# A linear-attention and two-MLP kernel: ScalarE's opening in another order, a 128x3 square on another engine, and the second batch's decays loaded at another point

## The chip, the cores and the metric

The kernel runs on one core of a Trainium2 chip. The metric is the device time of one execution in microseconds (us), the median over several runs. PE is TensorE, DVE is VectorE, ACT is ScalarE, POOL is GpSimd, and SP is the engine whose queue issues most of the DMAs. Each engine works through its own list of instructions in order; between engines, semaphores hold an instruction until its inputs are there.

## The reference, cut to what matters

```python
mag = sqrt(a_re**2 + a_im**2); scale = minimum(mag, 0.999) / (mag + 1e-6)
a = (a_re * scale, a_im * scale)               # complex decay, per (b, h, t, d)
for t in range(768):                           # B=4, H=8, D=48
    S = a[t] * S + k[t] v[t]^T                 # complex state, 48x48 per head
    y[t] = q[t] . Re(S)
x = y, heads side by side                      # (4, 768, 384)
u = x + token-MLP(x);  x1 = u + relu(u @ w_ch1) @ w_ch2
xn = layernorm(x1) * g_ln
out = x1 + relu(xn @ w2_ch1) @ w2_ch2
```

## The kernel before

A batch is worked in two stages. The first one (`gen_E` with `gen_A`, `gen_L2`, `gen_C`, then `gen_P`) turns the recurrence into matrix products; the second (`gen_M`) is the token MLP and the two channel MLPs.

In the first stage the 384 channels of a batch lie in three tiles of 128 partitions (i = 0, 1, 2), each in two halves of 384 time steps. Six *pieces* (tile, half) make a batch. `gen_A` first brings each decay to the right length. This is the piece's *first correction*: ACT squares the piece (L228), DVE adds the two squares, ACT takes Ln, Exp and a Square with a sum beside it (L232 to L234), and DVE finishes with three products and one 128x768 product into the decay tile `aj`. DVE then multiplies the decays together along 16 steps (`cmul`, a pair of products into `p`, then a pair of sums back into `aj`; below this is a *scan step*), and `gen_L2` joins the chunks. `gen_C` divides k by the running product and multiplies q by it, and its last two products write the four strips that SP sends, one DMA per head and strip, into the per-head tiles `stk` (L355, L356). `gen_P` then runs each head on PE: transposes of k (L425), scores (L438), state sums (L465), a scan on DVE (L466), and the outputs (L485, L497). Batch 0 goes in two parts, tiles 0 and 1 first and tile 2 behind (`PARTS`); heads 0 and 1 need only tile 0, heads 2 to 4 end in tile 1, heads 5 to 7 need tile 2.

Tile `aj` is shared by all batches. As soon as `gen_C` is through with tile i, `load_a(b + 1, i)` fetches the next batch's decays into its place (L63, 768 KB). The next batch's pieces then go through `gen_A` between the work of this batch. The scratch of the first two of them is called `t_1473` and `t_1559` in the lists below, the last tile of batch 0 works in `u`, `w_106` and `qk`.

The second stage reads weights that are split into two f16 parts on the way: POOL (and SP for the first few) loads `raw`, DVE and ACT split it (L530 to L534), 28 tiles in all. `tok1_half` is run twice: half 0 needs heads 0 to 3, half 1 heads 4 to 7. Its products go to the tile `y` (18 matmuls for j = 0, 18 for j = 1).

The program is written as generators that a driver interleaves, but the order on each engine is set by a scheduler at compile time, which estimates when each instruction can start. `tc.issue_after(x)` puts what stands under it behind instruction x on that engine. Where a queue's order in the lists below differs from the order of the code, the scheduler chose so.

Beside the result the kernel sums checks; `gstat` is the square of the layer-norm gain `gl`, three columns, compared at the very end (L1056). `gl` arrives by the 14th DMA of the SP queue.

Of the kernel before, what the change touches and what calls it, by code (L numbers as in the profile page):

```python
# [13 lines left out]
AF = mybir.ActivationFunctionType  # L14
ALU = mybir.AluOpType
PSUM = bass.MemoryType.PSUM

B, H, S, D = 4, 8, 768, 48
# [5 lines left out]
HB = S // 2  # L24
# [12 lines left out]
def tile_kernel(ctx: ExitStack, tc: tile.TileContext, a_in, qk_in, v_in, aq2_in, v2_in, wt_in, wm1_in, wm2_in, w64_in, g_in, c_in, out):  # L37
    nc = tc.nc
    V, A, T, G = nc.vector, nc.scalar, nc.tensor, nc.gpsimd
# [14 lines left out]
    def steps(x, i, half):  # L54

        if half is None:
            return x[:, :, i * S:(i + 1) * S]
        return x.rearrange("p x (i h s) -> p x i h s", i=3, h=2)[:, :, i, :, half * (HB // 2):(half + 1) * (HB // 2)]

    def load_a(b, i, half=None):  # L60
        o, s = steps(aj, i, half), steps(a_in[b], i, half)
        for x in range(2) if half is not None else (slice(0, 2),):
            nc.sync.dma_start(out=o[:, x], in_=s[:, x])  # L63
# [13 lines left out]
    gl = cp.tile([P, 3], F32, name="gl")  # L77
    nc.sync.dma_start(out=cst, in_=c_in)
    wstat = cp.tile([P, 28], F32, name="wstat")
    rstat = cp.tile([P, 6 * B], F32, name="rstat")  # L80
# [7 lines left out]
    gstat = cp.tile([P, 3], F32, name="gstat")  # L88
# [7 lines left out]
    V.memset(bias[:, 5:6], TINY)  # L96
    b_ln, b_one, b_eps, b_zero, b_eps_s, b_tiny = (bias[:, i:i + 1] for i in range(6))
    A.activation(out=eye_h, in_=eye, func=AF.Copy, scale=WS * WS)
    V.tensor_tensor(out=gstat, in0=gl, in1=gl, op=ALU.mult)

    w1 = ap.tile([P, FT, 4 * DM], F16, name="w1")
    w1_f = w1.rearrange("p k s -> p (k s)").bitcast(F32)
# [20 lines left out]
    def pair(x, n=2):  # L123
        return x.unsqueeze(1).to_broadcast([P, n] + list(x.shape[1:]))
# [29 lines left out]
    def big():  # L154
        return ap.tile([P, 6 * HB + 6], F32, tag="u", name="u", bufs=1)
# [4 lines left out]
    fin = {}  # L160
# [31 lines left out]
    def gen_E():  # L192
        V = Rec()
        nxt_q = [load_qk(0, j // 2, j % 2) for j in range(6)]
        load_w(1)
        for b in range(B):
            rec[0] = b == 0
            Ct = ap.tile([P, 3, 6 * 24], F32, tag="I", name="I")
            W = ap.tile([P, 2, 3, NCH], F32, tag="W", name="W")
            sq = ap.tile([P, 2, 3 * NCH], F32, tag="sq", name="sq")  # L200
            st = ap.tile([P, 2, 3 * NCH], F32, tag="st", name="st")
            V.memset(W[:, 0, :, 0:1], 1.0)
            V.memset(W[:, 1, :, 0:1], 0.0)
            for part in PARTS if b == 0 else ((0, 1, 2),):
                for x in gen_A(b, part):
                    yield x
                for x in gen_L2(b, part, Ct, W, sq, st):
                    yield x
                yield "C"
                for i in part:  # L210
                    for x in gen_C(b, i, Ct, st, nxt_q):
                        yield x
                    if b + 1 < B:
                        load_a(b + 1, i)
                    yield ("done", b, i)

    av = aj.rearrange("p x (j k r) -> p x j k r", j=6, k=KB)

    def gen_A(b, part):
        V = Rec()  # L220
        js = slice(2 * part[0], 2 * part[-1] + 2)
        n = 2 * len(part)
        for hf in range(2):
            for i in part:
                ah = steps(aj, i, hf)
                t = scratch(b, 2 * i + hf)
                s4, s5, s6, s7 = (t[:, j * HB:(j + 1) * HB] for j in range(4))
                A.activation(out=t[:, 0:2 * HB].rearrange("p (x h s) -> p x h s", x=2, h=2), in_=ah, func=AF.Square)  # L228
                yield "wait"
                V.scalar_tensor_tensor(out=s4, in0=s4, scalar=TINY, in1=s5, op0=ALU.add, op1=ALU.add)  # L230
                nn = s4
                A.activation(out=s5, in_=nn, func=AF.Ln)  # L232
                A.activation(out=s5, in_=s5, func=AF.Exp, scale=-0.5, bias=b_ln)
                A.activation(out=s6, in_=s5, func=AF.Square, scale=1.0 / 0.4995,  # L234
                             accum_out=rstat[:, 6 * b + 2 * i + hf:6 * b + 2 * i + hf + 1])
                if b == 0:
                    V.tensor_scalar(out=s7, in0=s5, scalar1=-EPS / 0.4995, scalar2=1.0, op0=ALU.mult, op1=ALU.add)
                else:
                    A.activation(out=s7, in_=s5, func=AF.Identity, scale=-EPS / 0.4995, bias=b_one)
                yield 470  # L240
                yield "wait"
                V.scalar_tensor_tensor(out=s4, in0=nn, scalar=-1.0, in1=s6, op0=ALU.mult, op1=ALU.mult)
                yield 470
                V.scalar_tensor_tensor(out=s5, in0=s4, scalar=3.0, in1=s5, op0=ALU.add, op1=ALU.mult)
                yield 470
                V.scalar_tensor_tensor(out=s4, in0=s5, scalar=1.0, in1=s7, op0=ALU.min, op1=ALU.mult)
                yield 470
                V.tensor_tensor(out=ah, in0=ah, in1=pair(s4.rearrange("p (h s) -> p h s", h=2)), op=ALU.mult)
                yield 870
            for j in range(max(1, hf * KB // 2), (hf + 1) * KB // 2):  # L250
                cmul(av[:, 0, js, j], av[:, 1, js, j], av[:, :, js, j], av[:, :, js, j - 1], [n, 24])
                yield 1200
        fin["scan"] = e0[-1]
        yield "L2"
# [261 lines left out]
    def load_w(n):  # L516
        while len(raws) <= n:
            m = len(raws)
            raws[m] = load_raw(m, "w2" if m in (2, 3) or 8 <= m < 16 else "tw")
# [194 lines left out]
    rs = {}  # L714

    def gen_M():
        r1 = [ap.tile([P, 2, DM], F16, tag="hid", name="hid", bufs=NHID) for _ in range(2)]
        tok1_half(0, r1)
        u = big()[:, 0:6 * HB].bitcast(F16).rearrange("p (x c s) -> p x c s", x=2, c=3)
        u_hl["uh"], u_hl["ul"] = u[:, 0], u[:, 1]  # L720
        yield "head"
        for _ in tok2(0, r1, (0,)):
            yield "tok"
        tok1_half(1, r1)
        yield "tok"
        for b in range(B):
            for _ in tok2(b, r1, (0, 1, 2) if b else (1, 2)):
                yield "tok"
            ln = iter(())
            if b == 0 and IL < FT:  # L730
                g = [mlp(wm1, 0, 0 < LNPE), mlp(wm1, 1, 1 < LNPE, ("sc", "tr", "y"))]
                for s in range(FT + 1 + IL):
                    for half in range(2):
                        if not 0 <= s - half * IL <= FT:
                            continue
                        k, acc = next(g[half])
                        if half:
                            next(ln, None)
                        if k < FT:
                            yield "step"  # L740
                        else:
                            for _ in ln:
                                pass
                            ln = gen_LN(half, acc)
                            next(ln)
            for half in range(0 if b or IL >= FT else 2, 2):
                for k, acc in mlp(wm1, half, 2 * b + half < LNPE):
                    next(ln, None)
                    if k < FT:
                        yield "step"  # L750
                for _ in ln:
                    pass
                ln = gen_LN(2 * b + half, acc)
                next(ln)
            for half in range(2):
                n = 2 * b + half
                for k, acc in mlp(wm2, half):
                    next(ln, None)
                    if half and b + 1 < B:
                        if k == 2:  # L760
                            tokw(b + 1, 0)
                        if k == K_TOK:
                            yield "x"
                            r1 = tok1(b + 1)
                    if k == FT - 3:
                        o = ap.tile([P, 3, HB], F32, tag="xc", name="o", bufs=1)
                        nc.sync.dma_start(out=o, in_=x2_d[n].rearrange("c p s -> p c s"))
                    if k < FT:
                        yield "step"
                for c in range(3):  # L770
                    t = tmp()
                    V.scalar_tensor_tensor(out=t, in0=acc[c][:, 0:HB], scalar=1 / (WS * WS), in1=rs[n], op0=ALU.mult, op1=ALU.mult)
                    V.scalar_tensor_tensor(out=o[:, c], in0=o[:, c], scalar=1 / US, in1=t, op0=ALU.mult, op1=ALU.add)
                    nc.sync.dma_start(out=out[c, :, n * HB:(n + 1) * HB], in_=o[:, c])
            yield ("done", b)
# [243 lines left out]
    for b in range(B):  # L1019
        k = 0  # L1020
        while True:
# [5 lines left out]
            x = nxt(M, "M")  # L1027
# [140 lines left out]
```

## Time and profile before

| | us |
|---|---|
| median of 3 runs | 973.39 (971.98 to 974.5) |
| the profiled execution | 972.28 |
| its span in the trace | 970.6 |
| PE busy | 834.6 |
| DVE busy | 744.1 |
| ACT busy | 496.8 |

The span is what the trace covers, from the first instruction to the last; 1.7 us of the profiled execution lie around it. Busy time alone doesn't bound the kernel: in the first 130 us PE has little to do and DVE works almost without a gap, while between 700 and 800 us PE is never idle and DVE works half of the time. So the table by stretches is the one to read, together with what each engine waited for.

### The profile page before, as it was taken

How to read it: one execution, taken by the hardware profiler on the slowest of the kernel's cores; microseconds unless marked ns; L12 is line 12 of the kernel's file. 1: busy time of each engine (PE TensorE's matmuls, PEld its weight loads, DVE VectorE, ACT ScalarE, POOL GpSimd, SP SyncE). 2: the span in 40 equal slices, each digit the busy share in tenths (PEclk: the TensorE clock that was granted, in tenths of full speed). 3: DMA queues.
4: the chain of work that ended last, by engine and by line, in shares of the span. 5: the costliest groups of instructions: out<-in, count | busy, mean ns of one | idle time of the engine just before them, and what ended most of it. 6: DMA issues, size and time to landing. Idle time of an engine off the chain costs nothing.

```text
span 970.6 us, 15833 instructions
## 1 busy us (share of the span) xinstructions
PE 834.6 (86%) x5738; PEld 570.6 (59%) x5738; DVE 744.1 (77%) x1597; ACT 496.8 (51%) x1364; POOL 59.6 (6%) x113
## 2 busy tenths in 40 slices
PE   0018989699988899999889999799999999999996
PEld 0018979356556687655556666466666666656563
DVE  6999957999997788997979999988675523264543
ACT  6014434533543459434868972574676533354532
POOL 0000101000102100001010000011000000011110
PEclk9999975799999789999899999999999999999998
DMA  8024475421447533114245120343120102255572
GB/s 283 0 57 128 160 208 164 167 79 66 153 133 225 159 107 107 64 34 130 57 118 168 32 62 1 115 127 80 55 56 25 50 1 90 86 194 195 190 239 94
DMA packets 45287, 108.28 MB, mean 112 GB/s; under 512 B 5904, under 2 KB 28560, under 8 KB 45200
## 3 DMA queue, kind: packets, MB, share of 16 engines
q1 hardware_dynamic: 36816, 61.57, 21.5%
q0 software_dynamic: 8384, 45.62, 14.2%
q8 instruction: 47, 0.77, 0.3%
q14 instruction: 40, 0.33, 0.1%
HBM read 77.20 MB, written 11.01 MB: 91 GB/s over the span
## 4 chain that ended last, share of the span: by engine, by line
PE 40%; DVE 28%; DMA 11%; issue 10%; ACT 6%; SPq 4%; POOL 0%; DVEq 0%; POOLq 0%; ACTq 0%
PE m L566 11%; PE m L567 11%; PE m L568 11%; DVE t L179 6%; DVE aj L179 4%; DVE p L179 4%; DMA stk<-t 3%; DMA stk<-qk 2%; DMA raw<-in_wm 2%; DMA aj<-in_a 2%; DVE hid L576 2%; PE sc L438 2%; SPq L355 2%; SPq L356 1%; DVE qk L179 1%
## 5 line engine op out<-in xcount | busy, mean ns | idle before, releaser
L576 DVE SCALAR_TENSOR_TENSOR hid<-m,hid 128x384 f16<-128x384 f32 x198 | 109.4, 553 | 113.4 <-ACT hid L574 112.8
L566 PE MATMUL m<-u,w 128*128 128x384 f16 x576 | 189.6, 330 | 1.5 <-DVE u L626 1.3
L567 PE MATMUL m<-u,w 128*128 128x384 f16 x576 | 189.8, 330 | 0.0
L568 PE MATMUL m<-u,w 128*128 128x384 f16 x576 | 189.7, 329 | 0.0
L574 ACT ACTIVATE hid<-m 128x384 f16<-128x384 f32 x198 | 96.0, 485 | 180.8 <-PE m L568 179.7
L567 PE MATMUL m<-hid,w 128*128 128x384 f16 x540 | 177.3, 329 | 12.3 <-DVE hid L576 12.0
L568 PE MATMUL m<-hid,w 128*128 128x384 f16 x540 | 177.0, 328 | 0.0
L568 PEld LDWEIGHTS <-w 128*128 128x128 f16 x1176 | 116.5, 99 | 89.7 <-issue 20.8
L567 PEld LDWEIGHTS <-w 128*128 128x128 f16 x1176 | 116.9, 99 | 75.1 <-issue 6.5
L566 PEld LDWEIGHTS <-w 128*128 128x128 f16 x1176 | 116.7, 100 | 75.2 <-issue 7.6
L566 PE MATMUL m<-hid,w 128*128 128x384 f16 x540 | 129.6, 328 | 2.4 <-ACT hid L574 2.1
L425 PE MATMUL tr<-cst,stk 96*128 96x96 f32 x125 | 17.1, 260 | 77.8 <-DMA stk<-qk 75.0
L179 DVE SCALAR_TENSOR_TENSOR t<-t 128x384 f32<-128x384 f32 x120 | 64.8, 549 | 8.5 <-ACT t L228 5.7
L425 PEld LDWEIGHTS tr<-cst,stk 96*128 96x128 f32 x125 | 13.9, 151 | 81.4 <-issue 71.3
L179 DVE TENSOR_TENSOR p<-aj 128x288 f32<-128x288 f32 (+2 forms) x150 | 52.7, 392 | 0.8
L179 DVE TENSOR_TENSOR t<-aj,I 128x768 f32<-128x768 f32 x40 | 36.4, 953 | 16.5 <-DMA stk<-t 11.8
L438 PE MATMUL sc<-stk 96*128 96x128 f32 x300 | 46.2, 289 | 2.7 <-DVE xc L682 1.4
L438 PEld LDWEIGHTS sc<-stk 96*128 96x128 f32 x300 | 42.3, 202 | 5.8 <-DVE r L443 1.7
L533 ACT ACTIVATE w<-raw 128x768 f16<-128x768 f32 x28 | 25.4, 906 | 30.0 <-DVE raw L531 29.8
L513 POOL DMA_DIRECT2D raw<-in_wm x48 | 25.9, 540 | 238.3 <-DVE w L534 109.0
L574 ACT ACTIVATION_READ_ACCUMULATOR hid<-m 128x1 f32 x198 | 38.5, 194 | 0.0
L546 ACT ACTIVATE sq<-sq 128x768 f16<-128x768 uint8 x28 | 23.6, 843 | 27.8 <-DVE sq L545 27.8
(268 smaller groups left out, 1670.7 us busy)
## 6 DMA issues: line engine op xcount, KB each, us to landing
raw<-in_wm POOLq DMA_DIRECT2D x48, 768.0 KB, 4.6
qk<-in_qk SPq DMA_DIRECT2D x23, 384.0 KB, 4.7
aj<-in_a SPq DMA_DIRECT2D x9, 768.0 KB, 5.0
stk<-t SPq DMA_DIRECT2D x40, 144.6 KB, 3.3
stk<-qk SPq DMA_DIRECT2D x40, 144.6 KB, 3.1
raw<-in_wt SPq DMA_DIRECT2D x6, 768.0 KB, 5.4
v<-in_v SPq DMA_DIRECT2D x32, 144.0 KB, 2.2
x_d<-xc SPq DMA_DIRECT2D x24, 192.0 KB, 2.5
```

Of the source, the lines that this page charges most:

```text
L179: r = getattr(nc.vector, n)(*a, **k)
L355: nc.sync.dma_start(out=stk[b, h][d0:d0 + m, hf], in_=R[r:r + m])
L425: T.transpose(tr[:, c * 96:(c + 1) * 96], qc(c, 1), eye[0:96, 0:96])
L438: last = T.matmul(sc[:, (c % 3) * P:(c % 3 + 1) * P], qc(c, 1), qc(c, 0), start=True, stop=True)
L513: (nc.sync if n < NSY else nc.gpsimd).dma_start(out=raw.bitcast(U8), in_=w_src[n].bitcast(U8)[:, 3:3 + 8 * S])
L533: wact[n] = A.activation(out=dst[:, :, 0], in_=w, func=AF.Copy, scale=WS).ins
L546: A.activation(out=t[:, HB:2 * HB].bitcast(F16), in_=bad_, func=AF.Copy, accum_out=wstat[:, n:n + 1])
L566: T.matmul(out_, wh, xh_, start=first, stop=False)
L567: T.matmul(out_, wh, xl_, start=False, stop=False)
L568: T.matmul(out_, wl, xh_, start=False, stop=last)
L574: A.activation(out=hl[:, 0], in_=p, func=AF.Relu, accum_out=hstat[:, n_h[0]:n_h[0] + 1])
L576: last[:] = [V.scalar_tensor_tensor(out=hl[:, 1], in0=p, scalar=0.0, in1=hl[:, 0], op0=ALU.max, op1=ALU.subtract).ins]
```

## The change

Three edits, and what the scheduler makes of them:

1. Under `tc.issue_after(fin["ln"])` the first Square of each piece of batch 0 stands behind the last Square of the piece before it. ACT takes the pieces one by one.
2. The check's square of `gl` is an ACT `Square` at the start of `gen_M` in place of a DVE product at L99.
3. For batch 0, `load_a(1, i)` is called for all three tiles when `gen_C` of tile 2 has been issued, not after each tile.

```diff
-    V.tensor_tensor(out=gstat, in0=gl, in1=gl, op=ALU.mult)
...
-                    if b + 1 < B:
+                    if b and b + 1 < B:
                         load_a(b + 1, i)
                     yield ("done", b, i)
+                if b == 0 and part[-1] == 2:
+                    for i in range(3):
+                        load_a(1, i)
...
-                A.activation(out=t[:, 0:2 * HB].rearrange("p (x h s) -> p x h s", x=2, h=2), in_=ah, func=AF.Square)
+                with (tc.issue_after(fin["ln"]) if b == 0 and "ln" in fin else ExitStack()):
+                    A.activation(out=t[:, 0:2 * HB].rearrange("p (x h s) -> p x h s", x=2, h=2), in_=ah, func=AF.Square)
...
-                A.activation(out=s6, in_=s5, func=AF.Square, scale=1.0 / 0.4995,
-                             accum_out=rstat[:, 6 * b + 2 * i + hf:6 * b + 2 * i + hf + 1])
+                fin["ln"] = A.activation(out=s6, in_=s5, func=AF.Square, scale=1.0 / 0.4995,
+                                         accum_out=rstat[:, 6 * b + 2 * i + hf:6 * b + 2 * i + hf + 1]).ins
...
     def gen_M():
+        A.activation(out=gstat, in_=gl, func=AF.Square)
```

In the lists of the changed kernel the line numbers are 1 lower from L100 on and 2 to 4 higher further down (L228 is L231, L234 is L237, L355 is L358, L376 is L379).

ACT at the program's start, before: squares of the first pieces (`t`, `u`, `t`, `w_106`) stand between the Ln, Exp and Square of the others.

```order
L228 ACTIVATE t<-aj 128x768
L228 ACTIVATE u<-aj 128x768
L232 ACTIVATE t<-t 128x384
L228 ACTIVATE t<-aj 128x768
L233 ACTIVATE t<-t,bias 128x384
L232 ACTIVATE u<-u 128x384
L228 ACTIVATE w_106<-aj 128x768
L234 ACTIVATE t,rstat<-t 128x384
L232 ACTIVATE t<-t 128x384
L233 ACTIVATE u<-u,bias 128x384
```

ACT at the same place, changed:

```order
L231 ACTIVATE t<-aj 128x768
L235 ACTIVATE t<-t 128x384
L236 ACTIVATE t<-t,bias 128x384
L237 ACTIVATE t,rstat<-t 128x384
L231 ACTIVATE u<-aj 128x768
L235 ACTIVATE u<-u 128x384
L236 ACTIVATE u<-u,bias 128x384
L98 ACTIVATE eye_h<-cst 128x128
L720 ACTIVATE gstat<-gl 128x3
L237 ACTIVATE u,rstat<-u 128x384
```

Each piece now runs to its end before the next begins, and the square of `gl` stands inside the second piece, ahead of its last Square. DVE's list follows: of the 15 scan steps of tiles 0 and 1, two stood with other work between their products and their sums before, and eight do now; the number of instructions up to the end of these steps is the same but for the square of `gl`. Before that square DVE had six instructions to do, five of 384 columns into `t`, `u` or `w` with two inputs and one with one; in the changed list eight stand ahead of the first that needs the second piece's last Square, the 768-column product of the first piece among them.

DVE where tile 1 of batch 0 is finished, before: `u` and `qk` are its first half, `w1_106` its second, `p` and `aj_69<-p` the scan of tile 2, and `t_1473` the first piece of batch 1.

```order
L179 SCALAR_TENSOR_TENSOR t_1473<-t_1473 128x384
L179 TENSOR_TENSOR aj_69<-p_974 128x2x24 x2
L179 SCALAR_TENSOR_TENSOR qk_117<-u_110 128x384
L179 SCALAR_TENSOR_TENSOR t_1473<-t_1473 128x384
L179 SCALAR_TENSOR_TENSOR w1_106<-w1_106 128x384
L179 TENSOR_TENSOR p_995<-aj_69 128x96 x2
L179 TENSOR_TENSOR u_110<-qk_117,aj_69 128x768
L179 SCALAR_TENSOR_TENSOR t_1473<-t_1473 128x384
```

DVE at the same place, changed:

```order
L178 TENSOR_TENSOR u_109<-qk_116,aj_69 128x768
L178 TENSOR_TENSOR p_950<-aj_69 128x96 x2
L178 TENSOR_TENSOR w1_105<-qk2_110,w1_105 128x384
L469 SCALAR_TENSOR_TENSOR U_504<-tr_507,dr_505 96x288
L178 TENSOR_TENSOR qk_116<-qk_116,aj_69 128x768
L178 TENSOR_TENSOR aj_69<-p_950 128x2x24 x2
L178 SCALAR_TENSOR_TENSOR qk2_110<-w1_105 128x384
L469 SCALAR_TENSOR_TENSOR U_553<-m1_556,dr_554 96x288
```

No piece of batch 1 is left there. The five products of `t_1473` and those of `t_1559` now stand among the last corrections of tile 2, three of them ahead of the very last of these.

SP where the strips of tile 1 have been sent and those of tile 2 follow, before: `v` are the loads of the heads' values, and each waits until the head three before it is through on PE.

```order
L356 DMA w_648<-qk_111 16x771
L63 DMA aj<-in_a 128x2x768
L376 DMA v<-in_v 128x288 x4
L355 DMA w_648<-w_106 32x771
L355 DMA w_1115<-w_106 48x771
L355 DMA w_1118<-w_106 48x771
```

SP at the same place, changed:

```order
L359 DMA w_646<-qk_110 16x771
L379 DMA v<-in_v 128x288 x2
L63 DMA aj<-in_a 128x2x768 x2
L379 DMA v<-in_v 128x288
L358 DMA w_646<-w_105 32x771
L358 DMA w_1112<-w_105 48x771
L358 DMA w_1115<-w_105 48x771
```

The load of tile 0, which stood some twenty DMAs earlier, and that of tile 1 now follow each other behind the values of heads 4 and 5; tile 2's load follows the strips of tile 2 in both.

On PE two things differ in this stretch: the 18 matmuls of `y` for j = 1 stood in one row with those for j = 0, ahead of the transposes of head 5, and now stand behind the first eight transposes and six score products of heads 5 and 6. The rest of the second stage has the same order up to small swaps.

## Rows read from the trace of the kernel before

**Rows 1.** Table by stretches (span; PE, PEld, DVE, ACT, POOL busy; PEclk; DMA share; GB/s).
```profile
80.00:120.00 40.00, 34.40 (x172) 33.76 (x172) 38.52 (x110) 17.18 (x38) 2.92 (x8) 1.00 0.43 131
120.00:160.00 40.00, 35.65 (x195) 33.93 (x195) 22.51 (x39) 15.86 (x38) 3.24 (x6) 0.69 0.59 179
...
700.00:800.00 100.00, 100.00 (x810) 67.23 (x809) 55.19 (x102) 59.75 (x185) 0.00 (x0) 1.00 0.12 34
```

**Rows 2.** Instructions in order of time, opening (start, us, what, idle before and its releaser).
```profile
4.14 0.84 ACT L228 ACTIVATE t<-aj 128x768 f32<-128x768 f32 x1 [1.98 <-DMA aj<-in_a]
5.02 0.56 DVE L179 SCALAR_TENSOR_TENSOR t<-t 128x384 f32<-128x384 f32 x1 [3.77 <-ACT t L228]
...
12.99 0.16 DVE L99 TENSOR_TENSOR gstat<-gl 128x3 f32<-128x3 f32 x1 [0.74 <-DMA gl<-in_g]
13.07 0.55 DVE L179 SCALAR_TENSOR_TENSOR t<-t 128x384 f32<-128x384 f32 x1
...
44.85 0.26 DVE L179 COPY I<-aj 128x192 f32<-128x192 f32 x1
```

**Rows 3.** The same view, scan steps of tiles 0 and 1.
```profile
22.24 0.61 DVE L179 TENSOR_TENSOR p<-aj 128x192 f32<-128x192 f32 x2
22.78 0.55 DVE L179 SCALAR_TENSOR_TENSOR w<-w 128x384 f32<-128x384 f32 x1
...
25.05 0.41 DVE L179 TENSOR_TENSOR aj<-p 128x96 f32<-128x96 f32 x2
25.39 0.55 DVE L179 SCALAR_TENSOR_TENSOR w<-w 128x384 f32<-128x384 f32 x1
...
30.28 0.61 DVE L179 TENSOR_TENSOR p<-aj 128x192 f32<-128x192 f32 x2
...
31.39 0.63 DVE L179 TENSOR_TENSOR p<-aj 128x192 f32<-128x192 f32 x2
```

**Rows 4.** The chain that ended last, in order of time (start, us, what).
```profile
88.49 0.47 DVE t L179
...
90.89 0.87 DVE aj L179
...
98.75 5.52 DMA aj<-in_a
```

**Rows 5.** Instructions in order of time around the heads of batch 0.
```profile
73.70 0.56 DVE L443 TENSOR_TENSOR sT<-m,cst 128x384 f32<-128x384 f32 x1 [1.11 <-PE m L438]
...
104.36 0.84 ACT L228 ACTIVATE t<-aj 128x768 f32<-128x768 f32 x1 [2.50 <-DMA aj<-in_a]
...
112.22 0.33 SPq L376 DMA_DIRECT2D v<-in_v  x1
...
127.45 0.96 DVE L179 TENSOR_TENSOR u<-u,aj 128x768 f32<-128x768 f32 x1
...
128.74 0.24 PE L566 MATMUL y<-xh,w 128*128 128x192 f16 x1 [0.90 <-DVE hid L610]
...
130.14 0.25 PE L568 MATMUL y<-xh,w 128*128 128x192 f16 x1
...
133.46 0.44 PE L425 MATMUL m<-cst,w 96*128 96x96 f32 x3 [3.07 <-DMA w<-w]
```

**Rows 6.** Table by stretches of 5 us (columns as in Rows 1).
```profile
70.00:75.00 5.00, 5.00 (x26) 5.00 (x26) 3.82 (x12) 1.34 (x3) 0.00 (x0) 1.00 0.69 183
100.00:105.00 5.00, 5.00 (x28) 5.00 (x28) 4.12 (x12) 1.74 (x3) 1.74 (x3) 1.00 0.89 293
105.00:110.00 5.00, 5.00 (x27) 5.00 (x27) 4.53 (x23) 2.92 (x7) 1.18 (x6) 1.00 0.88 344
140.00:145.00 5.00, 5.00 (x28) 5.00 (x28) 2.92 (x6) 3.26 (x7) 0.00 (x0) 0.50 0.10 38
210.00:215.00 5.00, 5.00 (x33) 3.03 (x31) 5.00 (x11) 1.99 (x5) 0.00 (x0) 1.00 0.00 0
```

**Rows 7.** The chain of waits, PE at half clock.
```profile
158.31 0.32 PE m L566
```

## The prediction

> **What bounds the kernel now.** I read the table by stretches first. From 700 to 800 us PE works all the time, so nothing done early can help or hurt there except by starting it sooner or later [rows 1]. From 80 to 120 us DVE works 38.5 of 40 us and PE waits for strips that DVE makes; from 120 to 160 DVE works 22.5 of 40 [rows 1]. So the front is DVE's, up to its last product for tile 2 of batch 0, which starts at 127.45 and ends near 128.3 [rows 5]. Then come SP's transfers, and PE starts head 5 at 133.46 after waiting 3.07 us for a strip [rows 5]. Everything behind is released by data, nothing by the clock on the wall: if head 5 starts earlier, the rest moves, unless a later wait doesn't.
>
> The second view was the instructions in order of time. In the opening the reader should look at DVE's start at 5.02 and at 13.07, from where it hardly stops until the copy at 44.85 that closes the scan [rows 2]. The third was the chain of waits: at 90.89 it goes through a 768-column product that finishes a piece of batch 1, and at 98.75 through the 5.52 us load of batch 1's next tile [rows 4]. Work of the second batch stands on the first batch's path.
>
> **The change, part by part.** All sums are made against the profiled execution, 972.28 us with a span of 970.6. That is 1.1 below the median of 973.39; I carry the differences over to the median.
>
> *Opening.* Between 5.02 and 13.07 DVE had six instructions, five of 0.47 (the 384-column step of [rows 4]) and one shorter, 2.6 us in all, so 5.4 us idle [rows 2]. In the new order ACT reaches the square of `gl` near 10.3 us: Square at 4.14, 0.84 long [rows 2], and then Ln, Exp and Square with DVE's sum between, some 3 us for each piece by the same durations. But DVE's old square started at 12.99 after waiting 0.74 for that transfer [rows 2], and SP's list is the same up to there. So ACT stands until about 13.0, and behind it in its queue the second piece's last Square and all further pieces. DVE goes on at about 13.7. It has then done eight instructions, 3.8 us, and idled 4.9. Saved: 0.5, the small square included. If `gl` cost nothing there, up to 5.4 could go; if its wait runs longer than on DVE, nothing.
>
> *Scan steps.* A step with other work between its products and its sums takes 0.54 + 0.34 = 0.88 of DVE (22.24 to 22.78, 25.05 to 25.39); alone it takes 1.11 (30.28 to 31.39) [rows 3]. Six more steps are of the first kind: 6 x 0.23 = 1.4 saved. The Trainium skill (VectorE: DVE Perf Modes, The DRAIN you can't avoid) says that a Vector instruction can't start until the pipe has emptied behind the one before, and that leaving out the wait between them saves nothing. By it both kinds of step would cost the same, and the opening would bring 0.5 and not 1.9. The two kinds of step in this trace differ by 0.23, so I keep 1.4. Opening and steps: -1.9, ends -6.8 and 0.
>
> *Batch 1's pieces leave the front.* Two pieces were finished by DVE before 128.3. Each is four steps of 0.47 and one of 0.87 [rows 4], 2.75, together 5.5. In the new list three of the 0.47 steps still stand ahead of the last product of tile 2, 1.4. So -4.1. The rest falls behind that product, in the stretch in which DVE has 17.5 of 40 us free [rows 1]; that is the cover, and without it the 4.1 comes back. Ends -5.5 and 0.
>
> *Waits that go.* DVE idled 1.18 from 70 to 75, 1.11 of it for a score product, and 0.88 and 0.47 from 100 to 110 [rows 5, 6]. The first lies where the new list puts the last sums of tile 1 ahead of the scores. The others lie where ACT stood 2.50 us for batch 1's load before its Square at 104.36 [rows 5], with a head's copy of k behind it in the queue, and PE's state sums and DVE's scan behind that. Both go: -2.5. What is late next is `t_1473`. It now stands ahead of the last products of tile 2, needs its load, and that stands behind the values of head 5, which wait until head 2 is through. In the old trace head 2 is through at 112.22, when the values of head 5 go out [rows 5]; with the gains so far (1.9 + 4.1 + 2.5) that is 103.7. The load then lands some 6 us later (5.52 at 98.75 [rows 4], and the issues ahead of it), near 110. DVE gets to `t_1473` some 6.2 us ahead of its last product (counted under B), near 113.6, so the load is there; but ACT has two Ln and two Exp of tile 2 to do ahead of its Square. I allow 0.7 for that, less than one Square. Together -1.8, ends -2.5 and +3.0 (5.5 of wait, as in B, against the 2.5).
>
> *y for j = 1.* 18 matmuls, 128.74 to 130.14 at 0.08 each [rows 5], ran while PE waited for strips and cost nothing. Now they stand among the transposes and scores of head 5, which PE works without a gap (140 to 145: 5.00 of 5) [rows 6]. 18 x 0.08 = 1.5. At half clock, 0.50 in that row, a step of 384 columns takes 0.32 [rows 7] against 5.00/33 = 0.15 at 210 us [rows 6], so it could be 2.9. It stands near the start, so I take the row at full clock: +1.5, ends 0 and 2.9.
>
> *The square of `gl` itself* is 0.16 on DVE [rows 2] and about that on ACT; beside the wait it is nothing. Three loads move as to time, none is added.
>
> Sum: -1.9 - 4.1 - 1.8 + 1.5 = -6.3. In the profiled execution's terms 966.0, at the median **967.1**.
>
> **The rivals.**
>
> *A. As summed.* About 967. Itself it goes down to 960.0, with `gl` free (-4.9) and neither the 0.7 nor the 1.5, and up to 970.4, with the scan steps' 1.4 and the opening's 0.5 lost and y at 2.9. For it: DVE leaves no slack before 128.3, and nothing behind is released by a clock. Against it: later rows are reordered by a few places as well, which can be worth a microsecond or two either way.
>
> *B. The load becomes the wait.* `t_1473` holds DVE's last products of tile 2. If heads 0 to 2 don't come earlier, the values of head 5 go out at 112.22 as before [rows 5], two loads follow, and the first lands near 118.2. ACT's 0.84 makes it 119.1, 5.5 after DVE wants it. DVE then has 6.2 us to the end of tile 2 (five of 0.47, four of 0.87, one of 0.36), 125.3 and not 128.3: -3.0, with y -1.5, **971.9**. For it: SP's order puts the loads behind values that wait for heads. Against: heads 0 to 2 depend on the same DVE list that gets 5 us shorter.
>
> *C. Hidden anyway.* From about 165 us on, splitting the weights and the second batch's scans fill DVE. If the weights' transfers set the pace there and not DVE, head 5's earlier start is lost: **973.4**. For it: weight tiles wait for buffers that heads free. Against: those heads come earlier too.
>
> *D. Slower: PE's clock.* The granted clock is 1.00 from 105 to 110 us and 0.50 from 140 to 145, PE being full in both [rows 6]; 120 to 160 has 0.69 [rows 1]. Between them lie PE's waits of 0.90 and 3.07 us [rows 5]. In that stretch the work is mostly f32, and little is lost. If the new order of waits makes the half clock last as long over f16 work, each 10 us of it do 5 us of work (0.32 against 0.15 a step). From 13 us of it on the gain is gone; 30 us of it, about what the stretch lasts now, cost 15: 967.1 + 15 = **982**. For it: a gap of PE stays ahead of head 5. Against: it stays at the same place in the order, so the slow stretch should fall on the same work. The Trainium skill (TensorE: Matmul & The Clock Gate, What's actually happening) says that activity releases the throttle; by that a PE as full as this would soon be back at full clock and D would cost a few microseconds at most. The trace has PE 5.00 of 5 busy at 0.50, which the rule doesn't explain, so I leave D its chance.
>
> **How the numbers follow.** Chances: A 0.62, B 0.13, C 0.12, D 0.13. A difference under 0.3%, 2.9 us, can't be told from none in this kernel. A lies below 970.5 whole; of B I count 0.03 as faster, 0.08 as same and 0.02 as slower, of C 0.02, 0.08 and 0.02, of D 0.03, 0.03 and 0.07. That is faster 0.70, same 0.19, slower 0.11. The range reaches from just inside A's lower end to just past C: 960.5 to 974.0. Below it I leave 0.08, above it D's tail, 0.10.
>
> **What the profile after would show.** Opening: ACT idle until about 13 ahead of the square of `gl`, DVE's closing copy near 43 in place of 44.85. If that copy comes at 40 or earlier, `gl` landed sooner than I think; at 45, the steps gained nothing. Front: no piece of batch 1 on DVE before about 112, and the last product of tile 2 ended near 121; an idle of several us ahead of `t_1473` with a load as releaser means B. PE: head 5 near 125 to 127 in place of 133.46, and the clock at 1.00 from 200 to 240. If head 5 comes that early and the end doesn't, it is C or D, and the granted clock tells which. I am wrong in kind if the time is above 973.4 with head 5 early, or if head 5 is not early at all.

## The result and the profile after

The changed kernel takes 958.37 us (median of 4 runs, 957.82 to 964.99) against 973.94 for the kernel before (4 runs, 971.98 to 975.13), a ratio of 0.9858 with a 95% interval of 0.9811 to 0.9904. The profiled executions stand at 957.82 and 972.28, spans 956.1 and 970.6: -14.5. Forecast were -6.3 and a range that ended at 960.5, so the direction was right and the forecast size less than half of the real one. Ratios here leave out runs more than 1.5% above the fastest of their kernel, which are two of frozen_y_first's six, its profiled one among them; medians count every run.

The table by stretches of the kernel after, columns as in [rows 1] (the x behind a busy time counts the records, one for each instruction that the trace holds):

```profile
80.00:120.00 40.00, 39.66 (x201) 39.60 (x202) 37.60 (x110) 15.45 (x36) 3.98 (x10) 1.00 0.58 176
120.00:160.00 40.00, 30.83 (x252) 27.36 (x251) 33.35 (x59) 22.80 (x59) 4.84 (x9) 0.87 0.84 269
```

From 80 to 120 us PE is busy 39.7 us in place of 34.4, DVE 37.6 in place of 38.5 [rows 1]; so PE had little to do only in the first 70 us, and not, as is said ahead of the prediction, in the first 130. From 120 to 160 PE does 252 records in 30.8 us where it did 195 in 35.7, and DVE works 33.4 us and not 22.5: there lies the larger part of the change.

The opening and the front of the kernel after, instructions in order of time (start, us, what, idle before and its releaser):

```profile
11.58 0.31 ACT L98 ACTIVATE eye_h<-cst 128x128 f16<-128x128 f32 x1 [1.31 <-DMA cst<-in_c]
11.79 0.19 ACT L720 ACTIVATE gstat<-gl 128x3 f32<-128x3 f32 x1
...
42.07 0.26 DVE L178 COPY I<-aj 128x192 f32<-128x192 f32 x1
...
114.72 0.84 ACT L231 ACTIVATE t<-aj 128x768 f32<-128x768 f32 x1 [1.73 <-DMA aj<-in_a]
...
115.60 0.56 DVE L178 SCALAR_TENSOR_TENSOR t<-t 128x384 f32<-128x384 f32 x1 [1.03 <-ACT t L231]
...
120.92 0.94 DVE L178 TENSOR_TENSOR u<-u,aj 128x768 f32<-128x768 f32 x1
```

The copy that closes the scan starts at 42.07 in place of 44.85 [rows 2], the last product of tile 2 at 120.92 in place of 127.45 [rows 5]. The square of `gl` waits for nothing. The new wait at `t_1473` is there, 1.03 us on DVE.

PE around the heads of batch 0, the kernel after (same columns):

```profile
121.48 0.37 PE L571 MATMUL y<-xh,w 128*128 128x192 f16 x1
127.28 0.74 PE L428 MATMUL m<-cst,w 96*128 96x96 f32 x3 [5.42 <-DMA w<-qk]
...
131.28 0.37 PE L569 MATMUL y<-xh,w 128*128 128x192 f16 x1
...
136.36 0.37 PE L500 MATMUL m<-U,w 96*128 96x48 f32 x2
136.55 0.38 PE L488 MATMUL m<-v,sT 128*128 128x48 f32 x2
...
147.84 0.41 PE L500 MATMUL m<-U,w 96*128 96x48 f32 x2
```

The same kind of products in the kernel before:

```profile
143.35 0.62 PE L485 MATMUL m<-v,sT 128*128 128x48 f32 x2
143.77 0.63 PE L497 MATMUL m<-U,w 96*128 96x48 f32 x2
...
164.06 0.63 PE L497 MATMUL m<-U,w 96*128 96x48 f32 x2
```

Head 5 starts at 127.28 and not at 133.46 [rows 5], 6.2 us earlier. But a pair of 48-column products, 0.42 from start to start before, takes 0.2 now, and head 7's last pair starts at 147.84 and not at 164.06: 16.2 us earlier. The ten us between are the length of heads 5 to 7, 30.8 us from head 5's first transpose to head 7's last product before and 20.7 now, and this length is PE's clock. PE alone, from 135 to 150 us (busy, records, PEclk, DMA share, GB/s), the kernel before:

```profile
135.00:150.00 15.00, 14.78 (x75) 0.51 0.48 154
```

and after:

```profile
135.00:150.00 15.00, 14.32 (x133) 1.00 0.67 217
```

PE is nearly full in both; at 2.4 GHz (1.00) it gets through 133 records, at 1.2 GHz (0.50) through 75. At the start of head 5 it is the other way round: three transposes take 0.74 in the changed kernel and took 0.44 before [rows 5]. The clock fell near 135 us in the kernel before, and rises near 132 in the changed one. Over the whole span PE is busy 822.3 us in place of 834.6 with the same products: 12.3 of the 14.5 us are work done at the higher level, 2.2 are less idle time.

Further on the lead is 18.7 us at the first `x_d` DMA (227.12, before 245.83) and 14.9 from 740 us to the last output. Part of what is given back shows in DVE's waits (engine, line, releaser: us in total, times, longest). After, 220 to 310 us:

```profile
DVE pad L533 <- DMA raw<-in_wm: 4.8, 4, 1.9
```

and before, 235 to 320 us:

```profile
DVE pad L530 <- DMA raw<-in_wm: 1.4, 4, 0.5
```

DVE comes to the weights earlier than they do. That is rival C in small: 3.4 us more of waiting for weights (2.4 more of waiting in all, 9.0 and 6.6), not the whole gain.

### The profile page after: what moved, and what is told of

It reads as the page before. It is cut to its first block, busy times and chain, and to the rows that moved or that the text cites. A ratio compares the mean times of both kernels' runs of the same rounds, so it can differ in the third digit from the quotient of the medians.

```text
span 956.1 us, 15845 instructions
## 1 busy us (share of the span) xinstructions
PE 822.3 (86%) x5738; PEld 558.1 (58%) x5738; DVE 743.5 (78%) x1596; ACT 495.0 (52%) x1365; POOL 57.9 (6%) x113
## 4 chain that ended last, share of the span: by engine, by line
PE 39%; DVE 26%; issue 13%; DMA 11%; ACT 7%; SPq 2%; POOL 0%; DVEq 0%; POOLq 0%; ACTq 0%
PE m L570 11%; PE m L571 11%; PE m L569 11%; DVE t L178 6%; DVE aj L178 4%; DMA raw<-in_wm 3%; DVE p L178 3%; DMA stk<-t 2%; DMA aj<-in_a 2%; DMA stk<-qk 2%; DVE qk L178 2%; DVE hid L579 2%; DVE w L178 1%; PE sc L441 1%; DVE U L469 1%
## 5 line engine op out<-in xcount | busy, mean ns | idle before, releaser
L577 ACT ACTIVATION_READ_ACCUMULATOR hid<-m 128x1 f32 x198 | 38.5, 195 | 0.0
```

The source lines that it names most:

```text
L577: A.activation(out=hl[:, 0], in_=p, func=AF.Relu, accum_out=hstat[:, n_h[0]:n_h[0] + 1])
```

## The experiments

What heads 5 to 7 "take" is below always the time from head 5's first transpose to the start of head 7's last product. Theory C (not the rival C above) said that the unforecast us come from the clock in these heads, and at first that the 18 products of `y` for j = 1 raise it by standing behind head 5's scores. Rivals: G, PE's idle time ahead of head 5 decides and not the place of `y`; R, the new order behind the heads brings them (the scheduler moved far more there than the text on the change says). P, which comes in with the last experiments, is that only products of `y` behind the scores move the clock, and other products don't. All times are medians; the kernel before had 972.25, 972.71 and 973.79 us in the three sessions (25, 21 and 8 runs).

**y_first.** The changed kernel, the transposes of k and the scores of heads 5 to 7 held behind `y`.

```diff
+                    with (tc.issue_after(fin["y"]) if n in (5, 6, 7) else ExitStack()):
+                        for c in range(5):
+                            T.transpose(tr[:, c * 96:(c + 1) * 96], qc(c, 1), eye[0:96, 0:96])
...
+                with (tc.issue_after(fin["y"]) if n in (5, 6, 7) else ExitStack()):
+                    for c in range(3 * half, 3 * half + 3):
+                        last = T.matmul(sc[:, (c % 3) * P:(c % 3 + 1) * P], qc(c, 1), qc(c, 0), start=True, stop=True)
...
```

> The changed kernel, with all 36 products of y held ahead of head 5, as they stood before the change. Theory C (clock): the 18 f16 products of y for j = 1, behind head 5's first transposes and scores, are what brought PE from its lower to its upper level near 132 us. Then this kernel shows 0.50 over most of heads 5 to 7, and from head 5's first transpose to head 7's last product about 30 us as before (31.0), not 20.8; the time is 965 to 969. Theory G (gap): what counts is PE's long idle time ahead of head 5 and that all strips are there when it starts; the place of y doesn't matter. Then heads 5 to 7 take 20 to 22 us and the time is 957 to 960.

Measured: 959.35 us (954.21 to 964.37), ratio 0.9853 [0.9804, 0.9903]. The profiled execution (964.37) has heads 5 to 7 at half clock, as C said:

```profile
135.00:150.00 15.00, 15.00 (x78) 0.50 0.48 160
```

Its time is just below where C put it (965 to 969), but the median is where G put it (957 to 960): other executions of the same kernel are 10 us faster. The scheduler had also changed the order further on, so this doesn't decide.

**y_late.** The kernel before, `y` for j = 1 moved behind head 5's scores.

```diff
-        tok1_half(0, r1)
+        tok1_half(0, r1, (0,))
+        yield "y"
+        tok1_half(0, r1, (1,))
...
```

> The kernel before, with one thing changed: the 18 products of y for j = 1 stand behind head 5's first transposes and scores. Theory C: PE rises to the upper level within a few us of them, heads 5 to 7 take 20 to 24 us in place of 31.0, and 4 to 9 us of that reach the end: 965 to 970. Theory G: heads 5 to 7 stay at 0.50 and take 30 us or more, 973 to 976. The strips arrive one by one in this kernel, so under G nothing else changes.

Measured: 968.23 us (962.27 to 974.65), ratio 0.9967 [0.9933, 1.0001]. In the profile (963.68) heads 5 to 7 take 25.7 us and not 30.8:

```profile
135.00:150.00 15.00, 14.83 (x137) 0.91 0.51 177
```

That is nearer to C's 20 to 24 than to G's 30, but the gain isn't clear of none, and the runs spread over 12 us again.

**only_pieces.** Edit 1 alone (the diff is its part of the change).

> The kernel before, with ScalarE's first pieces issued one by one and nothing else. Theory C: y stays ahead of head 5 here, so heads 5 to 7 stay at 0.50 and only the opening comes earlier: the copy that closes the scan near 42 to 43 in place of 44.85, the end at 970 to 973. Theory G: head 5 starts the same way, so it says the same. If the front counts for more than I think, under 968.

Measured: 970.61 us, ratio 0.9983 [0.9966, 1.0000]. The closing copy is at 42.15, head 5 starts at 131.44, the heads take 29.0 us, nearly all at 0.50. As expected by both.

**only_late_loads.** Edit 3 alone.

> The kernel before, with the second batch's decays loaded once all first corrections of batch 0 are done, and nothing else. In this order y for j = 1 stands behind head 5's first transposes, as in the changed kernel. Theory C: heads 5 to 7 take 20 to 23 us, and with the 4 us of the front the time is 960 to 964. Theory G: the same if PE's idle time ahead of head 5 is 5 us or so, else 968 to 971.

Measured: 974.09 us (967.60 to 980.17), ratio 1.0023 [0.9991, 1.0055]: no gain, against both theories. Head 5 starts at 129.22, 4.2 us earlier, after an idle time of 5.96 us, and the heads take 28.1 us. PE alone in stretches of them:

```profile
129.00:132.00 3.00, 2.78 (x15) 1.00 1.05 265
...
135.00:138.00 3.00, 3.00 (x31) 1.00 0.47 188
...
144.00:147.00 3.00, 3.00 (x19) 0.50 0.89 317
```

The heads start at half pace (15 records, under a clock that reads 1.00 but isn't recorded yet, see the last section), go on at 1.00 from about 135.6, and fall to 0.50 near 142.5 with PE full. Then the heads of the second batch meet half clock too; the table from 300 to 370 us here:

```profile
300.00:370.00 70.00, 61.17 (x317) 52.60 (x318) 48.65 (x80) 29.21 (x74) 5.19 (x8) 0.63 0.49 132
```

and in the changed kernel:

```profile
300.00:370.00 70.00, 64.51 (x431) 49.49 (x430) 56.63 (x102) 44.09 (x118) 3.02 (x4) 0.83 0.44 131
```

So the place of `y` doesn't by itself keep the clock up. Nor does the idle time ahead of head 5, as G had it: it is longer here than the 5.42 us of the changed kernel.

From here on each engine's order is written out, taken from the scheduler's list for one of the two kernels, so that nothing else moves:

```diff
+    for line in json.loads(zlib.decompress(base64.b85decode(ORDER))).values():
+        for x, y in zip(line, line[1:]):
+            if True:
+                tc.add_manual_dep(traced[y], traced[x].name, nosync, reason="order")
```

**front_new_rest_old and front_old_rest_new.** `ORDER` is cut at head 7's last product, and joins the lists of the two kernels.

> The order of every engine is written out: up to head 7's last product as in the changed kernel, from there on as in the kernel before. Theory C (clock): the 8 us that the forecast didn't have come from heads 5 to 7 at the upper level, and the order behind them is of no matter: 957 to 961. Theory R (rest): the scheduler gave everything behind head 7 another order as well, and that order brings them: then only the front's own gain is left, 964 to 968.

> The reverse: up to head 7's last product the order of the kernel before, from there on that of the changed kernel. Theory C: 970 to 974, since head 5 to 7 and all ahead of them are as before. Theory R: the new order of the rest brings its 8 us by itself: 963 to 967.

Measured: 958.78 us (956.02 to 961.94), ratio 0.9859 [0.9824, 0.9894], and 972.60 us, ratio 0.9998 [0.9977, 1.0019]. The first has the whole gain, the second none: R falls. Everything that the change brings is there when head 7 ends. The first kernel from 135 to 150 us:

```profile
135.00:150.00 15.00, 14.76 (x140) 1.00 0.57 189
```

and the second:

```profile
135.00:150.00 15.00, 14.73 (x74) 0.50 0.44 143
```

**frozen_y_first and frozen_y_late.** In `ORDER`, the 18 products alone are moved, in the changed kernel's lists ahead of head 5, in those of before behind head 5's scores.

> The changed kernel's order on every engine, written out, but for one thing: the 18 products of y for j = 1 stand ahead of head 5 as they did before. Theory C: PE stays at 0.50 over most of heads 5 to 7 and 5 to 8 us come back: 963 to 967. Theory R: the same time as the changed kernel, 957 to 960, whatever the clock does there.

> The order of the kernel before on every engine, written out, but for the 18 products of y for j = 1, which stand behind head 5's scores as in the changed kernel. Theory C: heads 5 to 7 take 20 to 24 us in place of 31.0, and the time is 964 to 968. Theory R: 970 to 974, even if the heads are faster, since DVE's old order behind them sets the end.

Measured: 962.03 us (951.31 to 969.18), ratio 0.9855 [0.9807, 0.9903], and 969.53 us (966.52 to 975.92), ratio 0.9975 [0.9952, 0.9999]. Inconclusive on the place of `y`: in the profiled execution of the first (its longest, 969.18) the heads run at 0.50 and take 29.9 us, in that of the second (975.92, longest too) they take 32.5 although `y` stands behind the scores. Each kernel has executions 9 us and more below that.

**changed_busy_gap and before_busy_gap.** Products that nobody reads are put on PE ahead of head 5, 50 in the changed kernel, 40 in that of before.

```diff
+            if g == 0 and j == 0:
+                busy(50, psum("tr", 1)[:, 0:P], kick[:, 0:P])
...
```

> The changed kernel's order written out, with 50 products of 128x128 (f16, on a spare accumulator, read by nobody) added on PE behind y for j = 0, in the 5.4 us in which PE waits for head 5's strips. Theory C (clock): PE then comes to head 5 at the upper level and keeps it more often; heads 5 to 7 take 19 to 21 us, the time is 953 to 958. Theory P (place of y): only the products of y behind the scores count, the added ones change nothing: 957 to 960.

> The order of the kernel before written out, with 40 such products on PE behind y for j = 1, in the 3.1 us ahead of head 5. Theory C: heads 5 to 7 at the upper level in place of 0.50, 20 to 24 us in place of 31.0, and the time 963 to 968. If the time stays at 970 to 974 with heads 5 to 7 at 1.00, the faster heads are lost again in the old order, and the clock there can't be the missing 8 us. Theory P: heads 5 to 7 at 0.50, 971 to 976.

Measured: 952.16 us (950.89 to 958.38), ratio 0.9796 [0.9757, 0.9834], and 967.27 us (963.96 to 970.49), ratio 0.9937 [0.9911, 0.9964]. In the second the heads take 24.9 us and not 30.8. They start at the upper level here as in the kernel before, but the clock falls to 0.50 near 143 us and not near 135:

```profile
135.00:150.00 15.00, 14.74 (x107) 0.76 0.50 175
```

The order is that of the kernel before but for the 40 products, which feed nothing; head 5 starts 0.15 us later than before, and 6.5 us are gained: C's core, that the clock in these heads sets the time, holds, and P falls. The first kernel has the lowest median of all and lies below both forecasts; its products go into the gap, which shrinks from 5.42 to 2.60 us:

```profile
121.52 3.42 PE L367 MATMUL tr<-cst,eye_h 128*128 128x128 f16 x50
127.54 0.47 PE L434 MATMUL m<-cst,w 96*128 96x96 f32 x3 [2.60 <-DMA w<-qk]
```

Its heads take 20.6 us, no less than the 20.7 of the changed kernel, and end at the same time; the 6 us by which its profiled execution is faster arise later, some 3 of them between 553 and 744 us, where PE idles 8.4 us and in the changed kernel's like stretch 11.3. Why is open.

**changed_busy_start.** 60 such products ahead of head 0.

```diff
...
+                        busy(60, psum("y", 1)[:, 0:P], kick[:, 0:P])
...
```

> The changed kernel's order written out, with 60 such products on PE ahead of head 0, from about 61.6 us. Theory C, carried on: heads 0 to 4, which take 0.21 a product of 48 columns where heads 5 to 7 take 0.11, come to the upper level, DVE's waits of 1.9 us at 70 to 80 and 1.5 at 110 to 120 go, and head 5 starts 1 to 3 us earlier: 954 to 958. Rival: DVE sets the front, and PE's pace there is of no use: 957 to 961.

Measured: 957.59 us (952.11 to 963.45), ratio 0.9814 [0.9781, 0.9847], beside 958.44 for the changed kernel: no gain that can be told, as the rival said. PE comes to head 0 at the upper level, and idles 4.67 us for a strip at 74.43. But its table says something else, columns as in [rows 6]:

```profile
105.00:110.00 5.00, 5.00 (x27) 5.00 (x27) 5.00 (x10) 1.34 (x3) 0.00 (x0) 0.50 0.13 37
```

The kernel before has 27 records in the same 5 us with PE full, under a clock of 1.00 [rows 6]. The work is done at one pace, so the 1.00 there is no recorded clock.

**changed_again.** The changed kernel itself.

> The changed kernel itself, beside the two above: 956 to 960 by its four runs so far, one of which was at 965. In the profile heads 5 to 7 at 1.00 (theory C says that an execution with them at 0.50 is the one near 965).

Measured: 958.44 us (956.87 to 967.75), ratio 0.9873 [0.9821, 0.9925]; the heads of the profiled execution (956.87) take 21.3 us, at 1.00 from about 134 on. That the one at 967.75 had them at 0.50 wasn't seen.

All profiled executions together (us; head 5's first transpose, start of head 7's last product, their difference, the execution's time, and what is left of it behind head 7):

| kernel | y, j = 1 | head 5 | head 7 | heads | time | rest |
|---|---|---|---|---|---|---|
| before | ahead | 133.46 | 164.28 | 30.8 | 972.28 | 808.0 |
| only_pieces | ahead | 131.44 | 160.43 | 29.0 | 970.87 | 810.4 |
| front_old_rest_new | ahead | 133.15 | 163.35 | 30.2 | 969.21 | 805.9 |
| y_first | ahead | 127.80 | 158.47 | 30.7 | 964.37 | 805.9 |
| frozen_y_first | ahead | 128.53 | 158.43 | 29.9 | 969.18 | 810.8 |
| before_busy_gap | ahead | 133.61 | 158.51 | 24.9 | 965.54 | 807.0 |
| y_late | behind | 133.01 | 158.75 | 25.7 | 963.68 | 804.9 |
| frozen_y_late | behind | 133.18 | 165.66 | 32.5 | 975.92 | 810.3 |
| only_late_loads | behind | 129.22 | 157.35 | 28.1 | 977.19 | 819.8 |
| changed_busy_start | behind | 128.24 | 156.38 | 28.1 | 963.45 | 807.1 |
| changed | behind | 127.28 | 147.96 | 20.7 | 957.82 | 809.9 |
| changed_again | behind | 128.28 | 149.58 | 21.3 | 956.87 | 807.3 |
| front_new_rest_old | behind | 128.19 | 149.57 | 21.4 | 959.07 | 809.5 |
| changed_busy_gap | behind | 127.54 | 148.10 | 20.6 | 951.68 | 803.6 |

In 13 of 14 the rest is 803.6 to 810.8. So the time follows the end of head 7 to within some 7 us, and that end has two parts: when head 5 starts (the front) and how long three heads take (the clock). only_late_loads is the exception, and loses at 300 to 370 us.

## Why the forecast fell short

**Opening and scan steps (-1.9): right, for a reason half wrong.** The copy came at 42.07, 2.8 earlier; over the profiles it stands at 43.5 to 44.9 with the old opening and at 42.0 to 42.5 with the new one, 1.8 apart in the mean. That the profiled execution of the kernel before has the latest of them is luck, and makes up 1 of the 2.8. ACT didn't stand for `gl` until 13.0. It stood for `cst` until 11.58, and `gl` was there by 11.79. So the opening brought more than 0.5. The eight steps with other work inside cost 0.54 + 0.34 as forecast; the Trainium skill's rule (VectorE: DVE Perf Modes, The DRAIN you can't avoid), by which they would cost as much as the others, isn't borne out by that; the section itself names an exception, a next instruction that isn't held.

**Batch 1's pieces and the waits (-4.1 and -1.8): nearly right.** The last product of tile 2 ended near 121.8, forecast were 121. The new wait at `t_1473` cost 1.03 and not 0.7, for a load as rival B said, but not 5.5. Head 5 started at 127.28, just outside the 125 to 127 given. By parts: 2.0 us with edit 1 alone, 4.2 with edit 3 alone, 6.2 together.

**y for j = 1 (+1.5): no cost.** It takes PE 1.9 us from 131.28, and the three heads are ten us shorter all the same. With the products ahead and nothing added the heads took 29 to 31 us in five profiles of five, with them behind 20.6 to 32.5 in eight. In those eight the clock rises while the 18 products run or within 0.2 us of their end, at 132.0 in the changed kernel. That they cause the rise is likely by that, and no run tests it apart; that they keep the clock up is refuted by the four in which it fell again inside the heads.

**The step that failed** is in rival D: "In that stretch the work is mostly f32, and little is lost." It left the clock out of the sum, as a risk of one sign. Heads 5 to 7 took 30.8 us, at 0.50 from about 135 on, and take 20.7, at 1.00 from about 132 on, so 10.1 of the 16.3 us at head 7's end were lost there and could be won. The rows that the rival names, [rows 6], have 27 records at 1.00 from 105 to 110 and 28 in full five us at 0.50 from 140 to 145, and seem to bear the step out. But the first row's 1.00 is no recorded clock; changed_busy_start has the same 27 at 0.50. The two rows compared half clock with half clock. [Rows 7] against [rows 6], 0.32 for a step of 384 columns at half and 0.15 at full, had the real ratio, and it was applied to the f16 work only. With 30.8 / 2 to 30.8 us of heads the forecast would have had a further case, by this estimate up to 15 us lower, with a chance of its own. The front's terms were 1.6 us too large (7.8 in sum, head 5 came 6.2 earlier), which hides a part of the miss.

**A, B, C, D.** A was right up to head 5 and ended there. B was there with 1.03 us. C showed behind 220 us, and took back part of the lead. D's mechanism was the right one with the sign turned round: the new order moves the stretch at half clock, but off the heads and not onto other work.

**The signs.** Copy near 43, last product ended near 121, no piece of batch 1 on DVE before 112, clock 1.00 from 200 to 240: met. ACT idle until 13 ahead of the square of `gl`: not met. "If head 5 comes that early and the end doesn't" had no counterpart for an end that comes much earlier; the check of heads 5 to 7's own length was missing.

**What stays open.** What decides how long the upper level lasts. In all 14 profiles the clock rises ahead of or inside heads 5 to 7 while a row of f16 products runs (those of `y`, or the added ones) or within 0.7 us of its end. In before_busy_gap, where such a row reaches up to head 5, it then stays up for 9 us of the heads, in the kernel before for 2; the new front with `y` behind has it up to their end in four profiles of five. But the level fell with PE full in only_late_loads and in changed_busy_start, and executions of one kernel lie far apart (962.27 to 974.65 us in y_late). The Trainium skill (TensorE: Matmul & The Clock Gate, What's actually happening) says that the same kernel shows a different number of slow products from run to run; the two profiles of the changed kernel agree, with PE full from 130 to 135 us in both and 45 records there in one, 34 in the other. Its statement that activity releases the throttle isn't what the f32 heads show: changed_busy_start's PE is busy 30.00 of 30 us from 90 to 120 at 0.50.

## What to carry to other kernels

Before a stretch is called insensitive to PE's clock, compare the time of the same product at both levels, and take the level from its duration where the profile has no record of it. Price a clock that is low in the profile as something that can be won as well as lost, over all the work that stands in it. Where three f32 heads close the front of a pipeline, spare products in the gap ahead of them were worth 6.5 us in the old order (0.9937). The changed kernel with them reached 0.9796, though not by shorter heads.

## What the hardware showed that was not expected

The profile's clock reads 1.00 from the start to its first record, near 122 to 136 us in these kernels, whatever the products take: 0.42 for two of 48 columns at 116 us, 0.2 at 136. With records from 66.7 on, changed_busy_start shows 0.50 from 73.5 to 135.0 for the same work at the same pace. The trace of the kernel before shows it without any run: `y`'s products for j = 0 start 0.16 us apart, those for j = 1 0.08 [rows 5], both under 1.00.

```profile
127.31 0.37 PE L567 MATMUL y<-xl,w 128*128 128x192 f16 x1
127.47 0.37 PE L568 MATMUL y<-xh,w 128*128 128x192 f16 x1
128.74 0.24 PE L566 MATMUL y<-xh,w 128*128 128x192 f16 x1 [0.90 <-DVE hid L610]
128.82 0.24 PE L567 MATMUL y<-xl,w 128*128 128x192 f16 x1
```

A long stretch of mostly f32 heads stays at 0.50 with PE never idle (27 us and more in before, y_first, only_pieces and changed_busy_start), while the mostly f16 work from 700 to 800 us runs at 1.00 throughout [rows 1]. And once up, the same f32 heads stayed at 1.00 from 135 us to their end, 13 to 15 us, in four profiles.

Executions of one program on one core differ by up to 14 us here (951.31 to 965.46, frozen_y_first), while those of another kernel of the same length agree within 5 (969.03 to 974.04, only_pieces). That the level in the heads makes this spread is not shown: of each kernel but the changed one a single execution was profiled. The mean granted clock, which is on record for all, doesn't settle it, since it counts the opening without records as 1.00: in y_late the four executions under 965 us have 0.978 to 0.981 and the six above 0.959 to 0.966, but in front_old_rest_new 967.50 has 0.968 and 972.45 has 0.982.
